# GpSimd's extra waits for VectorE's instructions ahead of it in the plan, taken out

## The chip, the core and the metric

One core of a Trainium2 chip runs the whole kernel. Its engines each work through an instruction queue of their own: TensorE (PE; its weight loads are shown apart as PEld), VectorE (DVE), ScalarE (ACT), GpSimd (POOL) and SyncE (SP), which issues nearly all DMAs. They keep step by semaphores. The metric is device time in microseconds for one execution.

## What is computed

An input `x` of 2048 tokens by 576 features is normalised to `xn`, and the output is `x` plus two branches on `xn`:

```python
# A: a spectral filter
X = rfft2(xn); y = irfft2(X * (w_r + 1j * w_i))
# B: a router with one expert of 64 for each token and each of 32 heads
q = xn @ w_q                       # split into q1, q2 of 128
i1 = argmax(q1 @ k1.T); i2 = argmax(q2 @ k2.T)
e = i1 * 8 + i2                    # the softmax over one candidate is 1
out = sum over heads of gelu(xn . u[e]) * v[e]
return x + A + B
```

## The kernel before

The Fourier transforms are matrix products. The tokens are split 64 x 32, so a two-dimensional transform is a pass over 64 (`dft128`), a pass over the features (`d_fwd`), a pass over 32 with twiddles (`s_fwd`), the multiplication by the filter (`s_mul`), and the way back (`s_inv` with `s_left` and `s_last`, `d_inv`, `fin`). Products in two halves of float16 (a high part and the rest) stand in for float32: ACT copies the high part out of PSUM, and DVE subtracts it and writes the rest (`AB<-banks,AB`, `ABL`, `lo<-banks,lo` in the profile).

The router's two products with `w_q` and the keys are folded into one matrix (`fold_part`, `fold_end`, `fold_last`), so scores are one matmul with `x`. The stages that matter most below, for pairs of token tiles `r` = 0 to 7:

- `x_t(r)`: loads a piece of `x` transposed into `xf`, scales it to float16 (ACT), and for `r` of 2 and more POOL subtracts to get the rest (`xT<-xf,xT`, 128 x 640).
- `scores(r)`: the matmul into PSUM, Gelu on ACT, a scaling of it on POOL (`MT<-MT,mk`), then on DVE a maximum over seven candidates (`mx<-banks`), a comparison with it (`w<-banks,mx`) and a product with weights (`w<-w,wt`).
- `route(r)` and `combine(r)`: a dozen small DVE instructions that turn the comparisons into an index and a sum of selected activations (`w<-w`, `MT<-w`, `w<-MT,iv`, `w<-w,MT` and others), nearly all between tiles in SBUF. POOL makes one subtraction at the end (`MT<-MT`, 128 x 128). The scratch of these stages is a view `RM` of the tile `MT`, so the profile names it `MT`.
- `s_mul(g)`: 16 groups. DVE reads PSUM and writes `t` (`t<-banks,wx,Wt`); for `g` of 4 and more ACT copies the other factor and POOL multiplies it (`t<-t,Wt`, 128 x 578); then POOL adds and subtracts into `y`, a view of the tile `U` (`U<-t,t`, two of 128 x 289).
- `d_inv(t)`: at the end, POOL combines halves (`A<-t`, and `t<-U` for six tiles) before `fin`.

All operations are first recorded in a plan (`_Plan.add`). Each is then issued by `_Plan.issue` in the order of a list written out in the file, `ORDER` (1230 entries), with a PSUM bank for each PSUM tile from the list `BANK`; nothing reorders them afterwards. An engine's instructions run in that order. The framework puts semaphore waits where an instruction's data ask for them.

On top of these, `issue` adds waits of its own. `add` marks an operation as `port` if it is POOL's with an input, or DVE's with its output in SBUF and two inputs in SBUF of more than one element a row (or a `tensor_copy` or `tensor_scalar` whose single tensor input is in SBUF). While issuing, `held` is the last marked DVE operation so far; each marked POOL instruction gets a wait for the end of that one, on top of its data's. As all of DVE's work up to `held` ends before `held` does, POOL so stands behind every marked DVE instruction ahead of it in the order. A marked DVE instruction that comes later in the order gets no wait for POOL from this.

Every instruction is issued by one line of `issue`, so all of them carry the line L321 in the profile; they are told apart by tiles and shapes.

Of the kernel before, what the change touches and what calls it, by code (L numbers as in the profile page):

```python
# [16 lines left out]
WAIT = mybir.DependencyInfo(mybir.DependencyClass.Sync, mybir.DependencyReason.DATA)  # L17
# [253 lines left out]
class _Plan:  # L271
# [42 lines left out]
    def issue(self, tc):  # L314
        for v, k in zip(self.tiles, BANK):
            v.slot = k
        held = None
        for i in ORDER:
            o = self.ops[i]
            for fn, args, kw in o.calls:  # L320
                o.last = fn(*[x.place() if isinstance(x, _Ps) else x for x in args],  # L321
                            **{k: x.place() if isinstance(x, _Ps) else x for k, x in kw.items()})
                if o.port and o.eng == "gpsimd" and held is not None:
                    tc.add_manual_dep(o.last.ins, held.last.ins.name, WAIT, reason="the shared port")
            if o.port and o.eng == "vector":
                held = o


def body(tc, nc, a, out):
# [799 lines left out]
```

## Time and profile before

| | us |
|---|---|
| median of 3 runs | 208.03 |
| lowest, highest | 204.81, 208.6 |
| the profiled execution | 205.82 |
| its span, first to last instruction | 203.8 |
| granted TensorE clock in it | 0.993 |

Busy in that span of 203.8 us: TensorE 190.8 us (94%), VectorE 159.5 (78%), ScalarE 124.1 (61%), GpSimd 105.7 (52%, 166 instructions). The DMA engines moved 44.13 MB.

How to read the rows that follow. In a timeline: start and duration in us, engine, line, operation, output<-inputs by the program's names, partitions x elements and type, how many instructions were merged into the row (x2), and in brackets the idle time before it and what ended it. In a list of waits: who waited for whom, total us, times, longest. In a table by stretch: start and end, length, then busy us (and instructions) of PE, PEld, DVE, ACT and POOL, then the granted clock, the DMA share and GB/s. PSUM tiles all appear as `banks`. A wait for several semaphores is put down to the one that came last.

### The profile page before, as it was taken

Reading aid. Unit: us, or ns where it says so; the run is one execution under the profiler, and the core shown is the slowest. Engines: PE = TensorE matmul, PEld = TensorE weight load, DVE = VectorE, ACT = ScalarE, POOL = GpSimd, SP = SyncE. Lnnn points to the kernel's source line nnn. Section 1 sums busy time; section 2 is a strip of 40 time slices with the busy share of each in tenths; the row PEclk is TensorE's granted clock in tenths of the full one; section 3 lists DMA queues with packets and bytes.
Section 4 is the critical chain, followed back from the end, with each engine's and each line's share of the span. In section 5 each row is a group of like instructions: output and inputs, shape, how many; then the busy total and the mean of one; then the engine's idle time right before and its main releaser. Section 6 shows DMA issues by size and latency. Waiting matters only on the chain.

```text
span 203.8 us, 6358 instructions
## 1 busy us (share of the span) xinstructions
PE 190.8 (94%) x2511; PEld 126.5 (62%) x2511; DVE 159.5 (78%) x383; ACT 124.1 (61%) x272; POOL 105.7 (52%) x166
## 2 busy tenths in 40 slices
PE   7877989999998999999999999999999999999990
PEld 2476787886675567754445554578454887777640
DVE  3899999855656556686998479899989998879862
ACT  3699988954736584879977651786540754333310
POOL 2573665100550064814337775833592549799841
PEclk9999999999999999999999999999999999999997
DMA  6999699999999989794557364512201000006585
GB/s 222 405 422 417 232 384 413 416 412 395 324 356 371 402 342 352 184 305 128 139 146 211 75 169 149 169 31 69 48 10 17 10 3 2 5 0 233 195 309 194
DMA packets 21155, 44.13 MB, mean 217 GB/s; under 512 B 7942, under 2 KB 10758, under 8 KB 21126
## 3 DMA queue, kind: packets, MB, share of 16 engines
q1 hardware_dynamic: 20838, 43.45, 59.8%
q8 instruction: 19, 0.31, 0.6%
q10 hardware_dynamic: 288, 0.30, 0.4%
q14 instruction: 10, 0.08, 0.1%
HBM read 38.30 MB, written 4.72 MB: 211 GB/s over the span
## 4 chain that ended last, share of the span: by engine, by line
PE 67%; DVE 12%; DMA 9%; issue 4%; ACT 3%; POOL 2%; SPq 1%; DVEq 0%; ACTq 0%; POOLq 0%
PE banks L321 67%; DMA Wt<-in_W_dram 4%; DMA XN<-in_x_dram 2%; DMA ABL<-lo 2%; DVE st L321 2%; DVE w L321 2%; DMA s<-in_s_dram 2%; DVE AB L321 2%; POOL xT L321 1%; DVE A L321 1%; DVE mx L321 1%; SPq L321 1%; DVE rr L321 1%; DVE t L321 1%; ACT MU L321 1%
## 5 line engine op out<-in xcount | busy, mean ns | idle before, releaser
L321 PE MATMUL banks<-MU,xT 128*128 128x512 f16 x192 | 44.4, 379 | 0.0
L321 PEld LDWEIGHTS <-xT 128*128 128x128 f16 (+1 forms) x240 | 20.7, 99 | 27.4 <-issue 5.0
L321 PEld LDWEIGHTS <-AB 128*128 128x128 f16 x400 | 31.2, 123 | 7.2 <-issue 3.3
L321 POOL TENSOR_TENSOR U<-t,t 128x289 f32<-128x289 f32 x32 | 21.7, 702 | 21.9 <-DVE sc L321 15.7
L321 PE MATMUL banks<-c,AB 128*128 128x145 f16 (+1 forms) x384 | 32.4, 228 | 0.3 <-DVE AB L321 0.3
L321 POOL TENSOR_TENSOR t<-t,Wt 128x578 f32<-128x578 f32 x12 | 15.6, 1315 | 22.5 <-ACT t L321 17.2
L321 DVE TENSOR_TENSOR AB<-banks,AB 128x512 f16<-128x512 f32 x32 | 21.7, 682 | 6.0 <-ACT AB L321 5.5
L321 POOL TENSOR_TENSOR xT<-xf,xT 128x640 f16<-128x640 f32 x12 | 16.8, 1404 | 16.2 <-ACT xf L321 5.9
L321 POOL TENSOR_TENSOR A<-t 128x289 f32<-128x289 f32 x32 | 21.4, 704 | 2.6 <-DVE MT L321 2.5
L321 PE MATMUL banks<-Rs,A 64*128 64x128 f32 x256 | 19.1, 288 | 3.2 <-ACT Rs L321 1.4
L321 ACT ACTIVATE AB<-banks 128x512 f16<-128x512 f32 x32 | 18.9, 596 | 3.8 <-PE banks L321 3.2
L321 PE MATMUL banks<-s,U 64*64 64x128 f32 x624 | 20.3, 272 | 0.0
L321 PEld LDWEIGHTS banks<-Rs,A 64*128 64x128 f32 x256 | 16.7, 194 | 5.7 <-ACT Rs L321 3.3
L321 PEld LDWEIGHTS banks<-s,U 64*64 64x64 f32 x624 | 17.8, 133 | 2.5 <-issue 1.1
L321 PE MATMUL banks<-A,s 64*64 64x289 f32 x256 | 18.8, 408 | 0.5 <-DMA s<-in_s_dram 0.3
L321 PE MATMUL banks<-w,KP 128*32 128x288 f32 x256 | 18.0, 411 | 0.7 <-DMA w<-in_wq_dram 0.7
L321 ACT ACTIVATE U<-banks,sc 128x290 f32<-128x290 f32 (+1 forms) x16 | 9.3, 596 | 14.1 <-PE banks L321 11.4
L321 DVE SCALAR_TENSOR_TENSOR t<-banks,wx,Wt 128x578 f32<-128x578 f32 x20 | 15.6, 813 | 2.9 <-PE banks L321 2.8
L321 PE MATMUL banks<-c,ABL 99*128 99x289 f16 (+1 forms) x64 | 15.7, 288 | 0.2 <-ACT A L321 0.2
L321 DVE SCALAR_TENSOR_TENSOR t<-banks,sc,U 128x290 f32<-128x290 f32 (+1 forms) x26 | 12.7, 527 | 3.4 <-ACT U L321 1.8
L321 ACT ACTIVATE t<-banks,wx 128x578 f32<-128x578 f32 x12 | 8.8, 744 | 10.5 <-DVE t L321 5.5
L321 ACT ACTIVATE xT<-xf,bx 128x640 f16<-128x640 f32 x16 | 13.1, 828 | 3.3 <-DMA xf<-in_xT_dram 3.0
(133 smaller groups left out, 349.3 us busy)
## 6 DMA issues: line engine op xcount, KB each, us to landing
w<-in_wq_dram SPq DMA_DIRECT2D x32, 576.0 KB
xf<-in_xT_dram SPq DMA_DIRECT2D x16, 320.0 KB
Wt<-in_W_dram SPq DMA_DIRECT2D x8, 578.0 KB
XN<-in_x_dram SPq DMA_DIRECT2D x7, 578.0 KB
out_dram<-XN SPq DMA_DIRECT2D x14, 288.0 KB
s<-in_s_dram SPq DMA_DIRECT2D x16, 192.0 KB
c<-in_c_dram SPq DMA_DIRECT2D x1, 868.5 KB
ABL<-lo SPq DMA_DIRECT2D x42, 16.5 KB
```

Of the source, the lines that this page charges most:

```text
L321: o.last = fn(*[x.place() if isinstance(x, _Ps) else x for x in args], **{k: x.place() if isinstance(x, _Ps) else x for k, x in kw.items()})
```

## The change

The waits that `issue` adds are taken out: `held` and the call that adds a dependency go. The order, the tiles, the banks and every operation stay, and the waits that the data ask for stay. 158 POOL instructions are marked (131 of the kind `TENSOR_TENSOR`, 14 `COPY`, 13 `TENSOR_SCALAR`); all but the first few carry an added wait before.

```diff
     def issue(self, tc):
         for v, k in zip(self.tiles, BANK):
             v.slot = k
-        held = None
         for i in ORDER:
             o = self.ops[i]
             for fn, args, kw in o.calls:
                 o.last = fn(*[x.place() if isinstance(x, _Ps) else x for x in args],
                             **{k: x.place() if isinstance(x, _Ps) else x for k, x in kw.items()})
-                if o.port and o.eng == "gpsimd" and held is not None:
-                    tc.add_manual_dep(o.last.ins, held.last.ins.name, WAIT, reason="the shared port")
-            if o.port and o.eng == "vector":
-                held = o
```

## The prediction

> **What bounds the kernel now.** I read the page first (busy times, chain), then the busy times by stretch, then what GpSimd (POOL) waits for, and last the order of time of VectorE (DVE) and POOL around those waits.
>
> ```profile
> PE 190.8 (94%) x2511; PEld 126.5 (62%) x2511; DVE 159.5 (78%) x383; ACT 124.1 (61%) x272; POOL 105.7 (52%) x166
> PE 67%; DVE 12%; DMA 9%; issue 4%; ACT 3%; POOL 2%; SPq 1%; DVEq 0%; ACTq 0%; POOLq 0%
> ```
>
> ```profile
> 118.00:137.00 19.00, 19.00 (x241) 10.85 (x234) 18.02 (x39) 10.49 (x21) 11.94 (x15) 1.00 0.45 132
> 137.00:158.00 21.00, 20.98 (x220) 11.87 (x217) 19.86 (x51) 9.12 (x18) 12.01 (x14) 1.00 0.17 41
> ```
>
> TensorE (PE) is the bound on average, and POOL is on 2% of the chain. The stretches say more. After the stretch and its length stand PE, weight loads, DVE, ScalarE (ACT) and POOL: from 118 to 158 us PE is busy all the time (19.00 of 19.00, 20.98 of 21.00) and DVE nearly so (18.02, 19.86). There two engines are the bound together, and POOL is busy little more than half. What POOL wins there is worth nothing; what DVE loses is worth its full length as soon as PE stands behind DVE.
>
> ```profile
> POOL t L321 <- DVE w L321: 7.0, 2, 5.2
> POOL U L321 <- DVE w L321: 3.9, 1, 3.9
> POOL xT L321 <- DVE MT L321: 3.8, 1, 3.8
> POOL MT L321 <- DVE w L321: 3.2, 1, 3.2
> ```
>
> These waits of POOL (total, times, longest) end with DVE writing `w` or `MT` in `scores`, `route` and `combine`, which `t`, `U`, `xT` and the scaled activation do not read. They are the extra waits, and the places where the change can act; part of each is a true operand that came little earlier. The early folds have a few of about 2 us at most. At most of its other instructions POOL is late already when the awaited DVE instruction ends.
>
> **What the change removes, and what it lets loose.** No computing instruction goes, and none moves in its queue. POOL starts earlier at the places above. Whether that costs something hangs on what POOL and DVE do to each other:
>
> ```profile
> 95.71 1.41 POOL L321 TENSOR_TENSOR xT<-xf,xT 128x640 f16<-128x640 f32 x1 [0.92 <-DVE mx L321]
> 96.80 0.80 DVE L321 TENSOR_TENSOR w<-w,wt 128x896 bf16<-128x896 bf16 x1
> ...
> 130.39 1.35 POOL L321 TENSOR_TENSOR U<-t,t 128x289 f32<-128x289 f32 x2
> 131.13 0.82 DVE L321 TENSOR_TENSOR w<-w 128x384 bf16<-128x384 bf16 x1
> ```
>
> ```profile
> L321 DVE TENSOR_TENSOR AB<-banks,AB x32: 627/684/692, 13.2 to 163.6; 128x512 f16<-128x512 f32 x32
> L321 DVE TENSOR_TENSOR w<-w x16: 284/320/825, 97.6 to 162.7; 128x384 bf16<-128x384 bf16 x8, 128x256 bf16<-128x256 bf16 x8
> L321 DVE TENSOR_TENSOR w<-w,MT x16: 394/418/425, 99.4 to 174.1; 128x512 bf16<-128x512 bf16 x16
> L321 DVE TENSOR_TENSOR w<-w,wt x8: 614/618/798, 96.8 to 161.0; 128x896 bf16<-128x896 bf16 x8
> ```
>
> (The three figures are minimum/median/maximum in ns.) `w<-w,wt` takes 0.62 us, but 0.80 when it starts at 96.80 under a POOL instruction that ends at 97.12: it ends at 97.60, 0.48 after POOL. `w<-w`, at most about 0.35 free (the median over both widths is 0.32), takes 0.82 under a POOL pair that ends at 131.74: it ends at 131.95, 0.21 after POOL. So a DVE instruction with two SBUF inputs stands until POOL is done and then needs its own time less **0.14 us**. `AB<-banks,AB`, with one input in PSUM, runs 0.63 to 0.69 throughout: such instructions pay nothing. The columns of `w<-w,MT` (0.39 to 0.43) show the other side of the waits: not one of 16 met a POOL instruction. Who is next when both engines want to go on is seen in one place:
>
> ```profile
> 84.63 1.56 POOL L321 TENSOR_TENSOR U<-t,t 128x289 f32<-128x289 f32 x2
> 84.93 0.71 DVE L321 TENSOR_SCALAR MT<-MT,mm__95 128x576 f32<-128x576 f32 x1
> ```
>
> A free pair of `U` takes 1.35 (row of 130.39); here it takes 1.56, and DVE ends at 85.64, long before the pair's end at 86.19. So DVE, waiting under the first `U`, went in **between two POOL instructions that follow each other**, and the second waited. I take it that this holds both ways: a waiting POOL instruction goes in between two of DVE's. That is the choice on which the forecast rests.
>
> The Trainium skill, page "SBUF — State Buffer", section "Who interferes with whom", calls this an exclusive lock that the loser waits out for a whole instruction; its section "A bandwidth-pool intuition that's wrong (but worth ruling out)" puts about 115 ns on top of the holder's end. By that figure each of the eight collisions below would cost 0.25 us more than I charge, an estimate of 2 us in all; the two rows above speak against it, since there the loser is quicker after the holder's end, not slower.
>
> **Step 1: 121 to 125 us.**
>
> ```profile
> 120.42 0.69 POOL L321 TENSOR_TENSOR U<-t,t 128x289 f32<-128x289 f32 x1
> 124.36 0.46 POOL L321 TENSOR_TENSOR MT<-MT,mk 128x128 f32<-128x128 f32 x1 [3.25 <-DVE w L321]
> 124.77 1.40 POOL L321 TENSOR_TENSOR xT<-xf,xT 128x640 f16<-128x640 f32 x1
> 126.13 1.32 POOL L321 TENSOR_TENSOR t<-t,Wt 128x578 f32<-128x578 f32 x1
> 127.40 0.47 POOL L321 TENSOR_TENSOR MT<-MT,mk 128x128 f32<-128x128 f32 x1
> ...
> 135.56 1.40 POOL L321 TENSOR_TENSOR xT<-xf,xT 128x640 f16<-128x640 f32 x1 [3.81 <-DVE MT L321]
> ```
>
> ```profile
> 118.25 1.09 DVE L321 TENSOR_REDUCE mx<-banks 128x128 f32<-128x896 f32 x1 [4.01 <-PE banks L321]
> ...
> 121.62 0.18 DVE L321 TENSOR_SCALAR MT<-MT 128x16 int32<-128x16 f32 x1
> 121.71 0.62 DVE L321 TENSOR_TENSOR w<-w,wt 128x896 bf16<-128x896 bf16 x1
> ...
> 123.46 0.76 DVE L321 TENSOR_TENSOR w<-w,MT 128x512 bf16<-128x512 bf16 x2
> ...
> 134.31 0.76 DVE L321 TENSOR_TENSOR w<-w,MT 128x512 bf16<-128x512 bf16 x2
> ...
> 136.30 0.41 DVE L321 TENSOR_TENSOR lo<-banks,lo 128x256 f16<-128x256 f32 x1
> ```
>
> POOL is free at 121.11 and today stands until 124.36, the end of DVE's run from 121.62 to 124.22 (nearly all with two SBUF inputs). Without the wait `MT` (0.46) runs beside the reduction before 121.62 at no cost. Then `xT`, `t` and the second `MT` (1.40, 1.32, 0.47) go in between DVE's instructions: 1.26 + 1.18 + 0.33 = **2.77 us** on DVE. Today the same three lie under DVE instructions that read PSUM, and are free.
>
> **Step 2: 134 to 137 us.**
>
> ```profile
> 133.51 0.82 ACT L321 ACTIVATE xf<-xf,bx 128x640 f32<-128x640 f32 x1
> ...
> 136.89 0.55 PE L321 MATMUL banks<-c,AB 128*128 128x145 f16 x6
> ```
>
> The `xT` of 135.56 has its input from ACT at 134.33. It would go in behind the first of the pair `w<-w,MT` at 134.70 and end at 135.95; the second then ends 0.28 later, at 136.23 and not 135.07: **1.16 us**. Against that the 0.47 us of today's collision at 131.13 (0.82 less 0.35) go, since POOL's work before it has moved. DVE is thus 2.77 + 1.16 - 0.47 = 3.46 us later at `lo` of 136.30. Nothing takes that up: DVE's rows follow each other without a gap of weight from 118.25 on. `lo` ends at 136.71, and the matmul at 136.89 goes into the PSUM bank that `lo` reads, 0.18 later. So PE is later by 3.46 - 0.18 = **3.3 us**.
>
> **Step 3: the other places.**
>
> ```profile
> 107.00 1.09 DVE L321 TENSOR_REDUCE mx<-banks 128x128 f32<-128x896 f32 x1 [0.23 <-PE banks L321]
> ...
> 109.77 0.69 DVE L321 TENSOR_TENSOR AB<-banks,AB 128x512 f16<-128x512 f32 x1 [0.55 <-ACT AB L321]
> ...
> 110.73 0.38 PE L321 MATMUL banks<-wm,on 128*128 128x2 f32 x2
> ```
>
> An `xT` that now goes ahead at about 105 costs DVE 1.26; idle time of 0.23 and 0.55 takes up 0.78 of it, and PE's distance behind `AB` (110.73 less 110.46) another 0.27: **0.2 us**. What a second `xT` costs at about 111 goes into the 4.01 us for which DVE waits at 118.25.
>
> ```profile
> 158.09 1.34 POOL L321 TENSOR_TENSOR U<-t,t 128x289 f32<-128x289 f32 x2 [3.89 <-DVE w L321]
> 158.29 1.09 DVE L321 TENSOR_REDUCE mx<-banks 128x128 f32<-128x896 f32 x1 [0.34 <-PE banks L321]
> 174.90 1.35 POOL L321 TENSOR_TENSOR A<-t 128x289 f32<-128x289 f32 x2 [1.31 <-DVE MT L321]
> ```
>
> The two `U` of 158.09 move under `route`: 2 x (0.67 - 0.14) = 1.06, less the idle 0.34: **0.7 us**. The two `A` of 174.90 move by 1.3 us under the last `combine`: again up to 1.06; part of them runs before it, and I take **0.8**. For the folds before 36 us I take nothing: the delays are a few tenths, and one of today's goes.
>
> Sum: 3.3 + 0.2 + 0.7 + 0.8 = **5.0 us**. The profiled execution took 205.82 us (span 203.8): 210.8. On the median of the three runs, 208.03, it is 213.0. I write **212**, between the two. 2% of the median is 4.2 us, and that is also about what a measurement of this kernel can tell from no change.
>
> The bounds of the price of a collision: below, POOL's instruction finds no gap in DVE's run and waits as today (nothing); above, its full length without the 0.14, for eight collisions 1.1 us more, and with the folds (0.5) and the second `xT` (0.8, through `U` to PE) 7.4 us. The row of 84.63 is nearest to the middle value, which I take.
>
> **The rivals.**
> *DVE keeps the pair.* If DVE's next instruction, issued before the last has ended (121.71 before 121.62 + 0.18), claims its place ahead of the waiting POOL, then POOL waits in hardware where it waited on a semaphore. Only `xT` at 121.6, which starts before DVE's run, still goes in: 1.26 - 0.47 - 0.18 + 0.2 = 0.8 us, so 206.6 to 208.8. For it: no row shows POOL going in between two DVE instructions. Against: the row of 84.63. It decides from the first DVE run that POOL meets.
> *An earlier POOL feeds PE.* PE waits little for POOL, and the chain's 2% at POOL are about 4 us; if a third of that were behind an extra wait, the kernel would gain 1.4 us: 204.4 to 206.6. Against: the long waits above end at DVE instructions that are themselves ahead of PE.
> *More than I charge*, the upper bound: 213.2 to 215.4.
> *The waits stay*, because a data dependency of the framework names the same DVE instruction: no change, 208.0.
>
> **How the numbers follow.** Forecast 0.46, DVE keeps the pair 0.24, POOL feeds PE 0.12, more 0.10, the waits stay 0.08. The forecast's own range, 209.5 to 213.5, lies for most of it over the 2%: slower 0.40 from it and 0.10 from the upper bound, 0.50; within 2% 0.46; faster 0.04, a part of POOL feeding PE. Range 205.5 to 216: only the fastest tail and what is past the upper bound are out.
>
> **What would show it.** Right: `w<-w,wt`, `w<-w`, `w<-MT,iv` and `w<-w,MT` with maxima of 1.2 us and more, DVE's busy time up by 4 us or more with the same instructions, POOL's waits for `w` and `MT` gone, and PE idle for DVE in 118 to 165. DVE keeps the pair: the POOL rows get longer instead, with the same ends as today. Wrong altogether: no row of either engine longer, for then the pair isn't contended as I read it.

## The result, and the profile after

The changed kernel takes **212.06 us** (median of 4 runs, 211.19 to 212.75; 206.72 for the kernel before in 4 runs beside it). The ratio is 1.0337, with a 95% interval of 1.0264 to 1.0409: slower. (The ratio leaves out two of those four runs of before, 208.03 and 208.6, as disturbed, and so rests on 204.81 and 205.41: against the median of all four it would be 1.026, and against 205.92, the median of 16 undisturbed runs of before taken with the first experiments, 1.030.) The profiled execution took 211.19 us with a span of 209.4; before it was 205.82 and 203.8.

The busy line of the page after:

```profile
PE 190.7 (91%) x2511; PEld 126.1 (60%) x2511; DVE 168.0 (80%) x383; ACT 124.3 (59%) x272; POOL 108.5 (52%) x166
```

The same 383 instructions of DVE now stand 8.5 us longer (159.5 before), POOL 2.8, the others are as busy as they were, and the span is 5.6 longer. The chain that ended last was followed back only part of the way in this trace (its shares add up to 39%), so I leave it out. The busy times from 118 to 137 us after:

```profile
118.00:137.00 19.00, 17.07 (x181) 8.72 (x184) 18.20 (x33) 9.49 (x18) 12.41 (x15) 1.00 0.43 131
```

Where PE was busy for 19.00 of 19.00 us, it is for 17.07; DVE is as full as before (18.20) with 33 instructions in place of 39. What POOL waits for, after:

```profile
POOL xT L320 <- ACT xf L320: 12.8, 6, 5.6
```

The four waits that the prediction listed are gone. What POOL waits for at these places now is its true operand, as in the row above; of its waits for DVE's `MT` one of 0.6 us is left. DVE's rows with their extremes (minimum, median, maximum in ns), by the tile `MT` before, then by the tiles `w` and `MT` after:

```profile
L321 DVE TENSOR_SCALAR MT<-MT x16: 163/170/323, 104.5 to 188.4; 128x16 int32<-128x16 f32 x16
L321 DVE TENSOR_TENSOR MT<-w x8: 217/220/226, 98.4 to 163.5; 128x128 bf16<-128x128 bf16 x8
...
L321 DVE SCALAR_TENSOR_TENSOR MT<-MT,sc x8: 339/346/352, 106.4 to 189.0; 128x128 f32<-128x128 int32 x8
```

```profile
L320 DVE TENSOR_TENSOR w<-w x16: 283/320/733, 97.0 to 166.4; 128x384 bf16<-128x384 bf16 x8, 128x256 bf16<-128x256 bf16 x8
L320 DVE TENSOR_TENSOR w<-w,MT x16: 393/417/691, 98.8 to 178.9; 128x512 bf16<-128x512 bf16 x16
...
L320 DVE TENSOR_TENSOR w<-w,wt x8: 614/708/1897, 96.2 to 164.7; 128x896 bf16<-128x896 bf16 x8
L320 DVE TENSOR_TENSOR MT<-w x8: 215/220/1421, 97.7 to 167.2; 128x128 bf16<-128x128 bf16 x8
```

```profile
L320 DVE TENSOR_SCALAR MT<-MT x16: 163/170/1340, 103.9 to 193.0; 128x16 int32<-128x16 f32 x16
...
L320 DVE SCALAR_TENSOR_TENSOR MT<-MT,sc x8: 334/344/1390, 106.9 to 193.6; 128x128 f32<-128x128 int32 x8
```

The minima and medians hardly move (only the median of `w<-w,wt` rises, from 618 to 708); but of four kinds a few rows have become 1.3 to 1.9 us long. Those rows, with POOL's beside them, in the order of time after (first POOL, then DVE):

```profile
104.20 1.42 POOL L320 TENSOR_TENSOR xT<-xf,xT 128x640 f16<-128x640 f32 x1 [1.12 <-ACT xf L320]
...
106.78 1.40 POOL L320 TENSOR_TENSOR xT<-xf,xT 128x640 f16<-128x640 f32 x1 [1.16 <-ACT xf L320]
...
122.18 1.39 POOL L320 TENSOR_TENSOR xT<-xf,xT 128x640 f16<-128x640 f32 x1
123.83 1.39 POOL L320 TENSOR_TENSOR t<-t,Wt 128x578 f32<-128x578 f32 x1 [0.26 <-POOL xT L320]
125.19 0.58 POOL L320 TENSOR_TENSOR MT<-MT,mk 128x128 f32<-128x128 f32 x1
...
136.03 1.54 POOL L320 TENSOR_TENSOR xT<-xf,xT 128x640 f16<-128x640 f32 x1 [2.65 <-ACT xf L320]
```

```profile
104.31 1.39 DVE L320 TENSOR_TENSOR MT<-w 128x128 bf16<-128x128 bf16 x1
...
106.94 1.39 DVE L320 SCALAR_TENSOR_TENSOR MT<-MT,sc 128x128 f32<-128x128 int32 x1
...
122.16 1.90 DVE L320 TENSOR_TENSOR w<-w,wt 128x896 bf16<-128x896 bf16 x1
123.98 1.28 DVE L320 TENSOR_SCALAR MT<-MT 128x16 int32<-128x16 f32 x1
...
125.38 0.54 DVE L320 TENSOR_TENSOR MT<-MT,fm 128x128 int32<-128x128 int32 x1
...
136.23 1.42 DVE L320 TENSOR_TENSOR MT<-w 128x128 bf16<-128x128 bf16 x1
137.58 1.03 DVE L320 TENSOR_TENSOR w<-w,MT 128x512 bf16<-128x512 bf16 x2
...
139.85 0.42 DVE L320 TENSOR_TENSOR lo<-banks,lo 128x256 f16<-128x256 f32 x1
```

Read the two side by side: each long DVE row begins with or just after a POOL row and ends a little after it (`w<-w,wt` at 124.06, the `xT` of 122.18 at 123.57), and POOL's rows come one between each two of DVE's, the `t` after the `xT`, the scaling after the `t`. `lo`, behind which PE stands, starts at 139.85; before it was 136.30.

**Where the 5 us come from, by place.** To see this without what differs from run to run ahead of it, I take the start of one DVE instruction at each border of a place, in every run, less its start before. The borders before are `w<-w,wt` at 103.59 and `t` at 192.01, with `mx` of 118.25 and `lo` of 136.30 between them:

```profile
103.59 0.62 DVE L321 TENSOR_TENSOR w<-w,wt 128x896 bf16<-128x896 bf16 x1
...
127.99 0.42 DVE L321 TENSOR_TENSOR lo<-banks,lo 128x256 f16<-128x256 f32 x1 [0.47 <-ACT lo L321]
...
192.01 0.65 DVE L321 SCALAR_TENSOR_TENSOR t<-banks,sc,U 128x290 f32<-128x290 f32 x1 [0.37 <-ACT U L321]
```

and after (with that of 139.85 above; the row of 130.54 is that of 127.99 before):

```profile
102.94 0.63 DVE L320 TENSOR_TENSOR w<-w,wt 128x896 bf16<-128x896 bf16 x1
...
118.63 1.09 DVE L320 TENSOR_REDUCE mx<-banks 128x128 f32<-128x896 f32 x1 [3.69 <-ACT xf L320]
...
130.54 0.42 DVE L320 TENSOR_TENSOR lo<-banks,lo 128x256 f16<-128x256 f32 x1
...
196.62 0.61 DVE L320 SCALAR_TENSOR_TENSOR t<-banks,sc,U 128x290 f32<-128x290 f32 x1
```

The shifts are -0.66, 0.38, 3.54 and 4.61 us (from starts before rounding). The change thus costs 1.04 us in 103 to 118 (place A), 3.16 in 118 to 136 (place B) and 1.07 in 136 to 192 (place C), **5.27 in all**; the other 1.0 us of the span's 5.6, and the 0.66 the other way, lie after and ahead of them. Nearly all of that 1.0 stands between DVE's last instruction and the end of the span (4.94 us, before 4.00). The run with 17 waits has 4.92 there and is no slower than before, so I don't put it down to the change. The table gives the same three numbers for the runs of the experiments, read in the same way from their profiled executions.

| kernel | median | ratio to before | at 103.59 | A | B | C |
|---|---|---|---|---|---|---|
| changed | 212.06 | 1.0337 [1.0264, 1.0409] | -0.66 | 1.04 | 3.16 | 1.07 |
| late waits only | 206.37 | 1.0022 [0.9982, 1.0061] | 1.82 | -0.19 | 0.00 | 0.02 |
| 17 waits | 206.79 | 1.0015 [0.9970, 1.0061] | -0.45 | 0.15 | 0.01 | -0.01 |
| 2 waits | 208.36 | 1.0140 [1.0086, 1.0194] | -0.53 | 1.20 | 0.01 | 0.98 |
| 4 waits | 207.62 | 1.0032 [0.9989, 1.0075] | 0.90 | -0.02 | 0.00 | 0.95 |
| waits dropped in B | 209.59 | 1.0196 [1.0141, 1.0252] | 0.19 | -0.30 | 3.04 | 0.04 |
| three filled | 209.18 | 1.0121 [1.0071, 1.0170] | -0.08 | 1.15 | 1.00 | 1.05 |
| seven filled | 208.69 | 1.0100 [1.0069, 1.0131] | 2.19 | -0.42 | -0.22 | 1.01 |
| `xT` twice | 215.36 | 1.0421 [1.0345, 1.0498] | 2.68 | 1.10 | 4.81 | 0.98 |

### The profile page after: what moved, and what is told of

The parts are those of the page before. It is cut to its first block, busy times and chain, and to the rows that moved or that the text cites. A ratio compares the mean times of both kernels' runs of the same rounds, so it can differ in the third digit from the quotient of the medians.

```text
span 209.4 us, 6351 instructions
## 1 busy us (share of the span) xinstructions
PE 190.7 (91%) x2511; PEld 126.1 (60%) x2511; DVE 168.0 (80%) x383; ACT 124.3 (59%) x272; POOL 108.5 (52%) x166
## 5 line engine op out<-in xcount | busy, mean ns | idle before, releaser
L320 PEld LDWEIGHTS <-xT 128*128 128x128 f16 (+1 forms) x240 | 20.8, 99 | 27.4 <-issue 4.8
L320 PE MATMUL banks<-Rs,A 64*128 64x128 f32 x256 | 18.9, 288 | 3.8 <-ACT Rs L320 1.5
L320 ACT ACTIVATE AB<-banks 128x512 f16<-128x512 f32 x32 | 18.9, 596 | 3.8 <-PE banks L320 3.3
L320 PE MATMUL banks<-A,s 64*64 64x289 f32 x256 | 18.1, 408 | 0.5 <-DMA s<-in_s_dram 0.5
L320 POOL TENSOR_TENSOR A<-XN 128x289 f32<-128x289 f32 x16 | 12.1, 766 | 5.6 <-DMA XN<-in_x_dram 3.9
```

## Experiments

My theory was that a POOL instruction and a DVE instruction with its inputs in SBUF exclude each other and take turns, so that POOL's work, once it no longer stands, costs DVE nearly its own length. The rivals: DVE keeps the pair of engines and POOL waits in hardware; what costs is another order of POOL's work (a buffer, a DMA, ScalarE) and the long rows only follow from it; and, for the size, that the loss comes from many small places, the early folds among them.

**The early waits.** Only the waits from place 375 of the order on, from `s_mul(0)`, are kept:

```diff
+FROM = 375
-        for i in ORDER:
+        for pos, i in enumerate(ORDER):
...
-                if o.port and o.eng == "gpsimd" and held is not None:
+                if o.port and o.eng == "gpsimd" and held is not None and pos >= FROM:
```

> The added waits stay for every POOL instruction from s_mul(0) on (52 us), and are gone from the folds and all else before it. Theory (VectorE pays for POOL instructions that go in between its own, and pays only where VectorE is ahead of TensorE, after 100 us): as before, within 1 us; of the 5.4 us nothing is left. Rival A (the loss begins early, by the order in which tiles and DMAs come free in the folds): 2 us or more above before. Rival B (every wait costs or saves a little, by its semaphore instruction): in proportion to the waits taken out, some 50 of 153, a third of the 5.4 us, 1.8 us.

206.37 us against 206.49 for before, ratio 1.0022. The waits of the layer norm and the folds are worth nothing that can be measured, so the loss is of the later ones. (The profiled execution of this run is 1.82 us late at 103.59, though its median is that of before; the run with seven filled comes back to this.)

**Two waits put back in place B**, those of the `MT` scaling of `scores(3)` and of the `xT` of `x_t(7)`, all others out:

```diff
+KEEP = (722, 824)
...
+                if o.port and o.eng == "gpsimd" and held is not None and i in KEEP:
+                    tc.add_manual_dep(o.last.ins, held.last.ins.name, WAIT, reason="the shared port")
```

> Of the 153 added waits two stay: that of the activation's scaling in scores(3) (124.36 us in the profile before) and that of the x_t(7) subtraction (135.56). Theory: steps 1 and 2 are given back, 3.2 us of the 5.4: 2 to 3 us above before. VectorE's w<-w,wt and MT<-MT of 122 to 124 us are back at 0.62 and 0.17 us. Rival (the loss is spread over all places, or comes from elsewhere): still 4.5 us or more above before.

208.36 us. The timeline of DVE in it:

```profile
122.38 0.62 DVE L323 TENSOR_TENSOR w<-w,wt 128x896 bf16<-128x896 bf16 x1
122.92 0.17 DVE L323 TENSOR_SCALAR MT<-MT 128x16 int32<-128x16 f32 x1
```

The two rows are at their free length again, and place B costs 0.01 us in place of 3.16. The long rows at 104 and 107 remain, and with them all of A and C.

**The opposite: the waits dropped in place B alone**, the 14 POOL instructions from place 769 to 905 of the order, `scores(3)` to `scores(5)`:

```diff
+FIRST, LAST = 769, 905
-        for i in ORDER:
+        for pos, i in enumerate(ORDER):
...
-                if o.port and o.eng == "gpsimd" and held is not None:
+                if o.port and o.eng == "gpsimd" and held is not None and not FIRST <= pos <= LAST:
```

> The other way round: all added waits stay, except those of the 14 POOL instructions from scores(3) to scores(5) (124.36 to 139.5 us in the profile before). Theory: 3.0 to 3.7 us slower than before, with w<-w,wt near 1.9 us and one MT<-MT of 16 elements near 1.3. Rival (a delay here is taken up later, where VectorE waits for TensorE at 150.0 and 158.3 us by 0.7 and 0.3): 2 us or less.

209.59 us; B costs 3.04 alone, and the rest -0.30 and 0.04. The timeline of DVE:

```profile
121.52 1.40 DVE L323 TENSOR_SCALAR MT<-MT 128x16 int32<-128x16 f32 x1
122.83 0.61 DVE L323 TENSOR_TENSOR w<-w,wt 128x896 bf16<-128x896 bf16 x1
123.36 1.28 DVE L323 TENSOR_SCALAR MT<-MT 128x16 int32<-128x16 f32 x1
...
135.62 1.42 DVE L323 TENSOR_TENSOR MT<-w 128x128 bf16<-128x128 bf16 x1
```

Here the small `MT<-MT` came first and paid for the `xT`, and `w<-w,wt` went free: which instruction pays is chance of a tenth of a microsecond, the sum is not. The loss of B here and those of A and C in the run before add up to the whole (3.04 + 1.20 + 0.98 = 5.22 us, against 5.27), and nothing is given back behind B. The ratios do so too (1.96% and 1.40% against 3.37%), but they were taken against different runs of before, so that this fits to the second decimal is luck.

**Which of the waits matter.** Only 17 of them are kept, those which by my reading of the trace of before are the last to end by a noticeable time:

```diff
+KEEP = (52, 20, 110, 130, 178, 236, 253, 489, 592, 667, 722, 824, 925, 990, 946, 1098, 1186)
-                if o.port and o.eng == "gpsimd" and held is not None:
+                if o.port and o.eng == "gpsimd" and held is not None and i in KEEP:
```

> Only the 17 waits stay that were the last to end for their POOL instruction in the profile before (23.5 us of POOL's idle time together); 136 go. Theory: as before, within 1 us, since the others were met before POOL came to them. Rival (the many waits that never show as idle time also keep POOL off VectorE's run, or cost time themselves): 1.5 us or more from before, either way.

206.79 us, ratio 1.0015, and 0.15, 0.01 and -0.01 in the three places. The other waits do nothing that can be measured.

**The pair by itself.** A kernel of ten stretches, each of equal instructions on both engines that start together.

> A kernel of its own that computes nothing of the reference: ten stretches in which POOL and DVE each run a row of equal instructions that start together, on tiles of their own. It shows the price of one collision and who goes next. My theory (a POOL instruction with inputs and a DVE instruction with its inputs in SBUF exclude each other for a whole instruction, and they take turns): POOL alone (128x640 subtraction to f16) 1.40 us each; DVE alone 0.42 for a product of 128x512 bf16 and 0.17 for the 128x16 scaling. Both together: a product takes 1.40 + 0.42 - 0.14 = 1.68 while POOL has work, one POOL instruction between two of DVE's; the small scaling about 1.3, as in the changed kernel at 123.98; the copy of 128x256 and the f32 product of 128x256 likewise their own time plus nearly a POOL instruction. With an input in PSUM (128x512) 0.69 as if alone, and the sum over groups of a row from SBUF likewise unchanged. With POOL filling a tile (no input): open, long rows if writing alone holds DVE off, 0.42 if not. Rival (DVE keeps the pair once it has it): after one wait of up to 1.40 all of DVE's rows stand at 0.42 back to back, and POOL's second row is longer by DVE's whole run. Rival (a fixed hand-over of about 115 ns on top of the holder's end): rows of DVE 1.40 + 0.42 + 0.1 = 1.9 or more.

DVE's rows (minimum, median, maximum) beside POOL's `xT`-like subtraction: a product (`dd`), the small scaling (`de`), a difference with an input in PSUM (`df`), a sum over groups of one SBUF input (`dg`); and the product beside fills (`dh`).

```profile
L46 DVE TENSOR_TENSOR dd<-dd x12: 425/1030/1636, 41.5 to 53.8; 128x512 bf16<-128x512 bf16 x12
L49 DVE TENSOR_SCALAR de<-de x12: 174/780/1396, 54.8 to 63.1; 128x16 int32<-128x16 f32 x12
L52 DVE TENSOR_TENSOR df<-ps,df x10: 690/691/692, 65.1 to 71.6; 128x512 f16<-128x512 f32 x10
L55 DVE TENSOR_REDUCE dg<-dg x6: 1219/1220/1222, 75.1 to 81.4; 128x32 f32<-128x1024 bf16 x6
L46 DVE TENSOR_TENSOR dh<-dh x16: 424/425/426, 85.2 to 92.1; 128x512 bf16<-128x512 bf16 x16
```

And the start of the stretch with products, in the order of time:

```profile
41.93 1.64 DVE L46 TENSOR_TENSOR dd<-dd 128x512 bf16<-128x512 bf16 x1
43.36 1.59 POOL L37 TENSOR_TENSOR pd<-pd 128x640 f16<-128x640 f32 x1
43.60 1.64 DVE L46 TENSOR_TENSOR dd<-dd 128x512 bf16<-128x512 bf16 x1
```

The two take strict turns: one POOL row, one DVE row, as long as POOL has work, with six rows of DVE at 1.63 or 1.64 and six at 0.42 or 0.43. DVE ends at 45.24, 0.29 after POOL's 44.95, and that is its own 0.43 less **0.14**, the number of the prediction. The Trainium skill, page "SBUF — State Buffer", section "A bandwidth-pool intuition that's wrong (but worth ruling out)", puts some 115 ns on top of the holder's end, measured there with DVE as the holder and a DMA that waits for GpSimd to write its descriptors. No run here shows that case; in these rows, where GpSimd holds and DVE loses, the loser is quicker after the holder's end, not slower. A product loses 1.64 - 0.43 = 1.21 us each time, while POOL's row grows only from 1.53 (alone) to 1.59. The hand-over saves time the other way, too: POOL's row ends at 44.95, 1.38 after the DVE row of 41.93 that it stood behind, and its own time is 1.53. The small scaling pays too (1.40), but two of them go through in one turn. An input in PSUM and a sum over groups cost DVE nothing beside a subtraction, nor do POOL's fills cost a product anything. Neither the rival in which DVE keeps the pair nor the fixed hand-over fits.

**Four waits**, the two of place B and those of the `xT` of `x_t(4)` and `x_t(5)`:

```diff
-KEEP = (722, 824)
+KEEP = (592, 667, 722, 824)
```

> The changed kernel with the waits of four POOL instructions put back: the two of the run before (scores(3) MT at 121 and x_t(7) xT at 135 us) and the xT of x_t(4) and x_t(5) at 104 and 107 us. My theory: my third step was sized too small because two xT, not one, met DVE there (rows of 1.39 at 104.31 and 106.94), which pushed mx and all behind it by some 1.0 us. So this kernel is 0.9 to 1.2 us faster than the one with two waits (208.4): about 207.3, ratio 1.003 to 1.008. What stays, some 0.7 us, is of the U and A after 155 us. Rival (the 104 us place is hidden in DVE's 4 us wait at 118, as I predicted for the second xT): 208.2 to 208.4, no change against two waits.

207.62 us, ratio 1.0032. A goes from 1.20 (two waits) to -0.02, so place A is settled: it isn't hidden in DVE's wait at 118. What stays is the 0.95 of C.

**POOL's work kept, its reading taken away.** In the changed kernel three POOL instructions of B are replaced by fills of their output:

```diff
+SWAP = (671, 815, 640)
...
+            if i in SWAP:
+                for k in range(2):
+                    o.last = o.calls[0][0].__self__.memset(o.calls[0][1][0], 0.0)
+                continue
             for fn, args, kw in o.calls:
```

> The changed kernel, without any extra wait, in which the three POOL instructions that DVE met at 122 to 125 us (the xT of x_t(5), the t of s_mul(10), the MT scaling of scores(2)) are each replaced by two fills of their output with zeros: the same places in POOL's queue, about the same time on POOL, but no input read. That part of the result is left out. In the run of pairs by themselves DVE's products stood at 0.42 throughout beside fills. My theory (what costs is the exclusion, not the earlier order of POOL's work): w<-w,wt is back at 0.62 (1.90 in the changed kernel), the two MT<-MT at 0.17 to 0.25 (0.24 and 1.28), MT<-MT,fm at 0.28 (0.54), and 2.5 to 2.7 us come back: 209.4 (209.0 to 210.0), ratio 1.011 to 1.018. Rival (POOL's work ahead of its place moves something else, a buffer, a DMA or ScalarE, and DVE's long rows are what follows): 211.5 to 212.5 as with the change.

209.18 us. No wait is there, POOL's queue has the same order, and the profile has:

```profile
122.83 1.34 POOL L323 MEMSET xT<- 128x640 f16 x2
...
122.86 0.66 DVE L326 TENSOR_TENSOR w<-w,wt 128x896 bf16<-128x896 bf16 x1
123.39 0.16 DVE L326 TENSOR_SCALAR MT<-MT 128x16 int32<-128x16 f32 x1
```

The time is as expected, the rows are free, and B costs 1.00 in place of 3.16. (The first small `MT<-MT`, at 122.69, was 0.83 long, but `w<-w,wt` started 0.17 behind it, so it cost DVE next to nothing; see the last experiment.) So at this place it is the exclusion that costs, not the order. That 2.2 us came back and not the 2.7 of the rows is explained below.

**Seven filled**, the `xT` of A and the one at 136 too:

```diff
-SWAP = (671, 815, 640)
+SWAP = (592, 596, 667, 671, 815, 640, 824)
```

> As the run with three, with the other POOL instructions that DVE met between 103 and 137 us filled too: the two xT of x_t(4), the xT of x_t(5) at 110, and the xT of x_t(7) at 136. No extra wait anywhere; that part of the result is left out. My theory: the rows at 104 and 107 (1.39 each) are back at 0.22 and 0.34, the pair w<-w,MT and MT<-w at 136 at 0.39 and 0.22, and only the U and A after 150 us are left, about 1 us: 207.2 to 208.0, ratio 1.003 to 1.009, the same as with four waits put back. Rival (the order of POOL's work): 209 or more.

A costs -0.42, B -0.22, C 1.01: at the places it is as expected. The whole, 208.69, is 0.7 over my upper end, and it is the median of ten runs: 2.3 us above the 206.38 of before, of which the three places make up 0.4. So what speaks against the order of POOL's work as a rival are the places, not the whole time. The profiled execution was 2.19 us late already at 103.59, ahead of all the fills. A part of that is PE's granted clock (third figure from the end), which was one half for a while:

```profile
17.50:20.50 3.00, 3.00 (x32) 3.00 (x32) 2.97 (x10) 2.37 (x7) 2.22 (x5) 0.50 1.02 412
```

The three executions that were 1.8 us late or more at 103.59 (this one, the late waits, `xT` twice) all have such a stretch, of 3.4 us, from about 17.4 to 20.8 us, and in all three DVE falls 0.67 or 0.68 us behind between the instructions that start at 18.9 and 26.2 us in the kernel before. Two others (the four waits, and the waits dropped in B) have it from 11.9 to 15.3 us and were only 0.90 and 0.19 late at 103.59; with the change, and before it, there is none so early. The rest of the shift, 1.1 to 2.0 us in the three, came between 26 and 103 us, and what sets it stays open, as does the 1.9 us by which the ten runs are slower than the places say. In the kernel with the late waits, one of the three, it isn't the edit: its median is that of before. One thing did not fit a clean picture: in this run and the one before it the small scaling stood at 0.66 and 0.83 until a fill ended, though products went free (but for one right behind a scaling, which ended with it). The last experiment settles that.

**`xT` twice.** In the changed kernel the `xT` of 122 us is issued two times:

```diff
+TWICE = (671,)
...
-            for fn, args, kw in o.calls:
+            for fn, args, kw in (o.calls * 2 if i in TWICE else o.calls):
```

> The changed kernel with the xT of x_t(5) at 122 us issued twice, one after the other. DVE's run of instructions on SBUF goes on from 122 to 128 there, so my theory (they take turns, so each POOL instruction more in such a run costs DVE its price) gives one more DVE row of 1.2 to 1.6 between 124 and 128 and 1.2 to 1.3 us more on everything behind: 213.3 (212.9 to 213.7), ratio 1.036 to 1.044. Rival (DVE takes a loss once for a run, whatever POOL holds ready): 211.9 to 212.3.

215.36 us, ratio 1.0421: the ratio is inside what I expected, the time 1.7 us above its upper end. The timeline of DVE shows one long row more, as the theory has it:

```profile
125.56 1.90 DVE L322 TENSOR_TENSOR w<-w,wt 128x896 bf16<-128x896 bf16 x1
127.38 1.37 DVE L322 TENSOR_SCALAR MT<-MT 128x16 int32<-128x16 f32 x1
...
128.86 1.39 DVE L322 TENSOR_TENSOR MT<-MT,fm 128x128 int32<-128x128 int32 x1
130.18 0.67 DVE L322 TENSOR_TENSOR w<-MT,iv 128x512 bf16<-128x512 bf16 x1
```

The excess over the free lengths is 1.28 + 1.20 + 1.11 + 0.25 = 3.84 us, where the changed kernel has 2.65: 1.2 for one more POOL instruction, as each turn costs. B costs 4.81, though, 1.65 more than with the change and not 1.2. The rest shows in PE's granted clock (third figure from the end) behind the place:

```profile
133.00:137.00 4.00, 3.04 (x50) 2.60 (x51) 3.63 (x6) 1.65 (x5) 2.96 (x4) 0.57 0.02 4
```

PE had been idle for 3.14 us for DVE's `t` until 133.96, and the clock was one half from 133.3 to 136.7 us, 0.57 in the mean of this stretch; in the changed kernel PE was idle for 1.93 there, and the clock stayed at 1.00. ACT's half of `lo` came later behind PE's restart, and DVE waited 0.37 us for that where the changed kernel doesn't. With this 0.37 the rows give 3.84 + 1.47 - 0.47 - 0.47 + 0.37 = 4.74 (the other terms are those of the next section). The rest of what separates this run from the changed kernel lies ahead of 103.59 (2.68 against -0.66), less 1.0 us behind DVE's last instruction, so its whole time says more than its edit does.

**Beside fills.** A second kernel of stretches, with POOL filling tiles:

> A kernel of its own that computes nothing of the reference, as the pair by itself, now with POOL filling tiles (an instruction that writes and reads nothing): six stretches in which both engines run rows of equal instructions that start together. Open is why a small scaling (MT<-MT, 128x16) stood at 0.83 and 0.66 beside fills while products did not. Theory 1: a DVE instruction with one SBUF input of this kind (scaling, copy) excludes any POOL instruction, and one with two SBUF inputs only a POOL instruction that reads. Then the scaling of 128x16 beside f32 fills of 0.63 and beside f16 fills has rows of 0.5 to 0.7 in place of 0.17, one in two or three of them, the copy of 128x256 rows of 0.6 to 0.9 in place of 0.29, and the f32 product of 128x256 and the bf16 product of 128x512 stand at 0.42 throughout, beside f16 fills too. Theory 2: a fill in f16 is another thing than one in f32. Then the scaling and the copy are free (0.17, 0.29) beside f32 fills, and the bf16 product is held up beside f16 fills (over 0.6). Theory 3: neither, the rows of that run waited for something else: 0.17, 0.29, 0.42 and 0.42 everywhere.

The small scaling beside f32 fills (`da`), and an f32 product with two inputs in SBUF beside them (`dd`):

```profile
L52 DVE TENSOR_SCALAR da<-da x16: 174/414/684, 15.8 to 22.8; 128x16 int32<-128x16 f32 x16
...
L61 DVE SCALAR_TENSOR_TENSOR dd<-dd x14: 424/426/427, 40.2 to 46.2; 128x256 f32<-128x256 f32 x14
```

While POOL had fills, the scaling took 0.65 to 0.68 in every row, in place of 0.17; beside f16 fills it was the same, and the copy rose from 0.29 to between 0.68 and 0.80. Products stood at 0.42 to 0.43 beside both kinds of fill. So there are two kinds of exclusion: these scalings and copies with one SBUF input exclude every kind of POOL instruction tried here, subtractions and fills, a product with two inputs only one that reads. That is theory 1, and every row that met a fill paid, not one in two or three. The Trainium skill, page "SBUF — State Buffer", section "Who interferes with whom", has the same two kinds, the first of them for copies and scalings in a mode that uses both of DVE's ports. The rows agree with it; that these ran in that mode no trace here shows.

None of these points to a kernel faster than the one before: 17 waits do what all of them do, and what they leave unguarded there is too little to be told from no change.

## Why the prediction was right, and where not

**The mechanism held.** The choice on which the forecast rested, that a waiting POOL instruction goes in between two of DVE's, is shown in the pair kernel, and with it the 0.14 of the hand-over. The rival in which DVE keeps the pair would have let a single `xT` in, the one at 121.6, and not five turns in B alone; the rival in which an earlier POOL feeds PE needed a place that gains, and with the change all three cost. The waits did go.

**Step 1 (2.77 us charged)**: the rows give 1.28 + 1.11 + 0.26 = 2.65. The instructions that paid were `w<-w,wt`, `MT<-MT` and `MT<-MT,fm`. The two POOL instructions that came by turns cost 0.07 less each than charged (1.11 for 1.18, 0.26 for 0.33); in step 1 I had taken the 0.14 of the hand-over off on DVE's side alone.

**Step 2 (1.16 us, less 0.47)**: the working let the `xT` end at 135.95, 1.25 us after the row of 134.70 that it goes in behind, where by its own rule of step 1 the price is 1.40 - 0.14 = 1.26 and not 1.16. What came: `MT<-w` paid first, 1.42 - 0.22 = 1.20, and the pair `w<-w,MT` behind it 0.27 (1.03 against 0.76): 1.47. POOL's scaling of the next scores, right behind the `xT`, took a turn as well, which I had not counted. The 0.47 of the old collision at 131 did go.

**What was missed between them.** I wrote that nothing takes up the loss because DVE's rows follow each other without a gap of weight. There is one: the row at 127.99 above stands 0.47 us for ACT's half of `lo`. After the change that wait is gone (the row of 130.54). With it the sum of B is 2.65 - 0.47 - 0.47 + 1.47 = 3.18, and 3.16 was measured; I had 3.46. It also explains the odd sum above: with three fills the 0.47 isn't used up, so B costs 1.47 - 0.47 = 1.00, and 2.2 us and not 2.65 came back. That PE follows DVE's `lo` is right, as PE's row shows:

```profile
140.31 0.28 PE L320 MATMUL banks<-c,ABL 99*128 99x289 f16 x1 [0.77 <-DVE lo L320]
```

**Step 3 is the term that was mis-sized.** For place A I charged one `xT` less all the idle time there, 0.2 us; it cost **1.04**. Two `xT` of `x_t(4)` met DVE, at 104.31 (1.39 - 0.22 = 1.17) and 106.94 (1.39 - 0.34 = 1.05), 2.22 in all; idle time and PE's distance took up 1.2. I had looked for the second one at about 111, where the `xT` of `x_t(5)` stands; that one did hide in the wait of 118.

For place C I charged 0.7 for the two `U` and 0.8 for the `A`, 1.5; it cost **1.07**. The `U` made `w<-w,wt` and `w<-w` longer (the 733 of the table of extremes), by 0.58 in all, but idle time took up all but 0.11 of it, 0.34 of that at 158. Two small scalings at 151.21 took a turn each with two `U` as well (1.27 together, 0.40 before), at a place that I had not charged; idle time took up all of that, most of it the 0.72 us for which DVE stood at 150.04 before. The `A` met one small scaling:

```profile
177.24 1.34 DVE L320 TENSOR_SCALAR MT<-MT 128x16 int32<-128x16 f32 x1
```

That is 1.17 over its 0.17, 0.96 of it on the path. The folds were charged nothing and cost nothing.

**So the sum came out by errors that cancel**: 0.1 too much in B (3.3 at PE), 0.4 too much in C, 0.8 too little in A, 5.0 against 5.27. That 212 was forecast and 212.06 measured is more luck still: 212 stood between two baselines, 205.82 and 208.03, and against the two runs of before in the ratio (205.1) the loss is 7.0 us, of which the places account for 5.27. Of the signs I named, DVE's busy time, POOL's waits and PE's idle time came; of the four maxima over 1.2 only that of `w<-w,wt` came (1.90), those of `w<-w`, `w<-MT,iv` and `w<-w,MT` did not (733, 424 and 691 ns). Other instructions paid in their place, in step 2 the one ahead of the one that I had named. The size doesn't depend on it, since POOL's instruction sets the price, whoever pays it.

## What to carry to other kernels

Where VectorE is with the bound and GpSimd is not, a GpSimd instruction that reads SBUF should run under VectorE instructions that read PSUM or that don't contend; one semaphore wait in the right place does that, and here four of the added waits carried 4.2 of the 5.3 us. Count the price in GpSimd's instruction length (here 1.1 to 1.3 us for 1.4), not in the length of the VectorE instruction that happens to stand. And when the price of a long row is carried to the end, look for each idle gap on the way, as it is used once.

## What the runs showed of the hardware

- The smallest instruction pays a whole turn: the scaling of 128x16, 0.17 us by itself, took 1.28 to 1.40 beside POOL. In the plan it counts as contending, in my list of those which would pay it was missing.
- Once the turn was missed: the scaling of 177.24 stood through two `A` of 0.69 and 0.68 us, although it was waiting when the first ended at 177.90. In the run with four waits the same two scalings took a turn each (0.68 and 0.73). I don't know what decides.
- A POOL fill reads nothing and still holds off DVE's scalings and copies (0.65 for 0.17), though not its products (0.42). A fill isn't always a free filler.
- PE's granted clock went to one half for stretches of 3.4 us. One began at 133.3 us in the run with `xT` twice, where PE had been idle for 3.14 us. But another began at 68.5 us of the same run, where PE had been idle for 1.19 us, and five executions have one from 11.9 or 17.4 us, near idle times of 1.0 and 1.5 us, which those without it have too; 1.93 us with the change was followed by none. So the length of one idle time doesn't tell when it comes. A long stall may cost more than its length: the mean clock of the four runs with `xT` twice is 0.969 to 0.983, that with the change 0.987 to 0.997. The Trainium skill, page "TensorE: Matmul & The Clock Gate", section "What's actually happening", has the clock fall to a half after an idle window of some 3.4 us. The stretches here are of that length; the idle times ahead of them are all shorter.
- At 103.59 us the profiled executions lie up to 3.3 us apart (-0.66 to 2.68) with the same instructions, if not the same waits, ahead of it; shifts between borders inside one execution told the places apart, to about 0.3 us in A and 0.05 us in B and C where the waits are as before, and whole times didn't.
